# Another order for the first chunks of a fused sparse-attention and squared-ReLU MLP kernel

## The chip, the cores and the metric

The kernel runs on one core of a Trainium2 chip. The metric is the device time of one execution in microseconds. The kernel before took 374.07 us, the median of three runs (371.66 to 374.30).

## The reference

Attention with two sparsity patterns is followed by a two-layer MLP. Inputs and output are float32; the sizes are 8 batches, 8 heads, 576 positions, head dimension 64, and 512 to 2048 to 512 in the MLP.

```python
rel = pos[:, None] - pos[None, :]
mask_local   = (rel >= 0) & (rel < 32)                          # heads 0 to 3
mask_strided = (rel >= 0) & (pos[None, :] % 32 == pos[:, None] % 32)   # heads 4 to 7
scores = np.where(mask, (q @ k.T) / 8, -1e9)
attn = softmax(scores) @ v
x = attn.transpose(0, 2, 1, 3).reshape(4608, 512)   # tokens x model
h = np.maximum(x @ moe_w_in, 0.0)
out = (h * h) @ moe_w_out
```

## The kernel before, in words

**Attention.** Heads are taken in pairs, so a batch has four units: unit 4b and 4b+1 are local (pairs 0 and 1), unit 4b+2 and 4b+3 are strided. Each unit goes through steps, and each step is a function that issues instructions on several engines:

- `step_T` (line 175): TensorE (PE) transposes q or k in 6 or 8 pieces into a PSUM tile `pt`; ScalarE (ACT, L188) copies q out, VectorE (DVE, L190) copies k out.
- `step_S` (line 214): PE makes the scores in four `pt` banks. ACT takes the exponentials (L220) in four pieces, the first at once and the others one, two and three groups later; DVE multiplies with the mask (L226).
- `step_D` (line 251): PE multiplies the weights with v and a column of ones, in two parts (local) or three (strided). DVE takes the reciprocal (L262) and scales (L263).
- `step_E` (line 274): PE transposes the result, and ACT (units below 12) or DVE copies it into `xt`, the MLP's input (L280, L282).

**MLP.** Tokens are cut into nine chunks of 512. `mm1(c, ff)` (L294) is four matmuls of 128x512 into a tile `ph`; ACT takes the ReLU (L297) and DVE squares it into `g_sb` (L298). `mm2(c, i)` (L309) is four matmuls too, a quarter of the sum for one output block of 128 tokens; after the fourth quarter ACT copies the block to `y` (L313) and SyncE (SP) sends it out (L315). Both kinds are called groups here. There are 288, and g0, g1 and so on number them in program order. The pool `ps_h` holds two `ph` banks, `ps_y` one `py` bank, `ps_t` five `pt` banks.

**Order.** It is written out by hand. `first_steps` does the attention of batch 0, with 5 small matmuls of the identity (L326, `warm`) after each step from the first `step_D` on. Then the list `groups` runs: MM1 of chunk 0 (g0 to g15), MM1 of chunk 1 (g16 to g31), MM2 of chunk 0 (g32 to g47), and from g48 MM1 of chunk c in turn with MM2 of chunk c-1. The table `due` says how many attention steps stand ahead of each group: the steps of batch 1 lie between g9 and g16, those of batch 2 between g28 and g48, those of batch 3 between g48 and g80, and so on with 32 groups for each batch. A chunk may start when the batches it touches are done: chunk 1 needs batch 1, chunk 2 needs batches 1 and 2, chunk 3 needs batch 3.

**Loads.** `loads(b)` issues a batch's loads: float32 q, k and v on SP's queue, and q and k of the strided units on GpSimd's (POOL's) queue, which converts to bf16 on the way. POOL then casts the float32 tiles (L95, L123, L124, L139), one after the other in program order, and waits there for each load. `loads(1)` stands after the attention of batch 0, `loads(2)` at g8, `loads(3)` at g16, `loads(4)` at g48. In `loads(1)` POOL also issues the four quarters of `w_out` (L148); the four quarters of `w_in` are issued earlier (L144). The first load of batches 1 and 2 has a gate: POOL first copies one element of `w_in` (its third quarter) or `w_out` (its third quarter) into the tile (L86), so the load waits until that quarter has landed.

Of the kernel before, what the change touches and what calls it, by code (L numbers as in the profile page):

```python
# [8 lines left out]
FP32 = mybir.dt.float32  # L9
# [5 lines left out]
def kernel(  # L15
# [9 lines left out]
    nc = tc.nc  # L25
    B, H, S, D = q.shape
# [25 lines left out]
    ps_h = ctx.enter_context(tc.tile_pool(name="ps_h", bufs=2, space=PS))  # L52
    ps_y = ctx.enter_context(tc.tile_pool(name="ps_y", bufs=1, space=PS))
# [26 lines left out]
    def load_qk_local(u, eng, gate=None):  # L80
        b, p = units[u]
        s = st.setdefault(u, {})
        for name, src in (("q", q), ("k", k)):
            t = qk_st.tile([QL, 2, 6 * D], FP32, name=f"{name}_st")
            if gate is not None and name == "q":
                nc.gpsimd.tensor_copy(t[0:1, 0, 0:1], gate)  # L86
            eng.dma_start(out=t, in_=src[b, 2 * p:2 * p + 2]
                          .rearrange("h (p j) d -> p h (j d)", j=6))
            s[name + "f"] = t

    def cast_qk_local(u, copies):
        s = st[u]
        for name, copy in zip("qk", copies):
            t = qk_in.tile([QL, 6, 2, D], BF16, name=f"{name}_l")
            copy(t.rearrange("p j h d -> p h j d"),  # L95
                 s[name + "f"].rearrange("p h (j d) -> p h j d", j=6))
            s[name] = t

    def load_qk_str(u):
        b, p = units[u]  # L100
        s = st.setdefault(u, {})
        for name, src in (("q", q), ("k", k)):
            t = qk_in.tile([SP_, 2, NJ * D], BF16, name=f"{name}_s")
            nc.gpsimd.dma_start(out=t, in_=src[b, 2 * p:2 * p + 2]  # L104
                                .rearrange("h (p j) d -> p h (j d)", j=NJ))
            s[name] = t

    def v_slot(u):
        b, p = units[u]
        return (b * 2 + p % 2) % NV  # L110

    def load_v_local(u, eng):
        b, p = units[u]
        t = vl_sts[p]
        for hh in range(2):
            eng.dma_start(out=t[32:128, NL * hh:NL * (hh + 1), :],
                          in_=v[b, 2 * p + hh].rearrange("(t p) d -> p t d", p=QL))
        st.setdefault(u, {})["vf"] = t

    def cast_v_local(u):  # L120
        s = st[u]
        t = vls[v_slot(u)]
        nc.gpsimd.tensor_copy(t[:, :, :, 0:D].rearrange("p h t d -> p (h t) d"), s["vf"])  # L123
        nc.gpsimd.tensor_copy(  # L124
            t[0:32, :, 1:NL, 0:D],
            s["vf"][96:128].rearrange("p (h t) d -> p h t d", h=2)[:, :, 0:NL - 1, :])
        s["v"] = t

    def load_v_str(u, eng):
        b, p = units[u]  # L130
        t = v_st.tile([SP_, 2, NJ * D], FP32, name="v_st")
        eng.dma_start(out=t, in_=v[b, 2 * p:2 * p + 2]
                      .rearrange("h (p j) d -> p h (j d)", j=NJ))
        st.setdefault(u, {})["vf"] = t

    def cast_v_str(u, copy=None):
        s = st[u]
        t = vss[v_slot(u)]
        (copy or nc.gpsimd.tensor_copy)(t[:, :, 0:D], s["vf"].rearrange("p h (j d) -> p (h j) d", d=D))  # L139
        s["v"] = t  # L140
# [15 lines left out]
    def run_due(test):  # L156
        due = [x for x in pending if test(x)]
        for x in due:
            pending.remove(x)
        for x in sorted(due, key=lambda x: x[0]):  # L160
            x[2]()
# [138 lines left out]
    ys = {}  # L300

    def mm2(c, i, pool=None):
        j, part = divmod(i, 4)
        g = gs[c]
        if part == 0:
            ys[c] = (pool or ps_y).tile([128, 512], FP32, name="py" if pool is None else "ph")
        py = ys[c]
        for ff in range(4 * part, 4 * part + 4):
            nc.tensor.matmul(py, g[:, ff, 128 * j:128 * (j + 1)], w_out_b[:, ff, :],  # L309
                             start=(ff == 0), stop=(ff == 15))  # L310
        if part == 3:
            y = y_pool.tile([128, 512], FP32, name="y")
            nc.scalar.copy(y, py)  # L313
            r0 = 512 * c + 128 * j
            nc.sync.dma_start(out=out[r0:r0 + 128, :], in_=y)  # L315
# [12 lines left out]
    def first_steps():  # L328
        order = []
        for u in range(3):  # L330
            order += [T_(u, "q"), T_(u, "k"), S_(u)]
        order.append(lambda: cast_v_str(2, nc.scalar.copy))
        order += [T_(3, "q"), T_(3, "k"), S_(3)]
        order += [D_(0, 0), D_(0, 1), D_(1, 0), D_(1, 1), E_(0)]
        for u in (2, 3):
            order += [D_(u, 0), D_(u, 1), D_(u, 2), E_(u - 1)]
        order.append(E_(3))
        n = len(order)
        return [(fn, 0 if i < 12 else 5) for i, fn in enumerate(order)]

    def stream_steps(lo, hi, base):
        order = [T_(lo, "q"), T_(lo, "k"), T_(lo + 1, "q"), S_(lo), T_(lo + 1, "k")]
# [22 lines left out]
    def loads(b):  # L365
        u = 4 * b
        for i in range(2):
            load_qk_local(u + i, nc.sync, gate=gates.get(b) if i == 0 else None)
            load_v_local(u + i, nc.sync)
        load_v_str(u + 2, nc.sync)  # L370
        load_v_str(u + 3, nc.sync)
        w_out = load_w_out if b == 1 else (lambda i: None)
        load_qk_str(u + 2)
        cast_qk_local(u, pool2)
        cast_v_local(u)
        load_qk_str(u + 3)
        cast_qk_local(u + 1, pool2)
        w_out(0)
        cast_v_local(u + 1)
        w_out(1)  # L380
        cast_v_str(u + 2)
        w_out(2)
        cast_v_str(u + 3)
        w_out(3)

# [53 lines left out]
    NCH = T // 512  # L439
    steps, ends = stream_steps(4, 8, 0)  # L440
# [4 lines left out]
    starts = {}  # L445

    def add(c, kind, i, pool=None):
        if kind == 1:
            if i == 0:
                starts[c] = len(groups)  # L450
            groups.append(lambda: mm1(c, i))
        else:
            groups.append(lambda: mm2(c, i, pool))

    for c in range(2):
        for i in range(16):
            add(c, 1, i)
    for i in range(16):
        add(0, 2, i, ps_h)
    for c in range(2, NCH):  # L460
        for i in range(16):
            add(c, 1, i)
            add(c - 1, 2, i)
# [2 lines left out]

    due = [0] * (len(groups) + 1)
    done_prev, g_prev = 0, 0
    for b in range(1, B):
        g_end, s_end = starts[b], ends[4 * b + 3]  # L470
        g_prev += 9 if b == 1 else 12 if b == 2 else 0
        for g in range(g_prev, g_end + 1):
            due[g] = done_prev + (s_end - done_prev) * (g - g_prev) // (g_end - g_prev)
        done_prev, g_prev = s_end, g_end
    load_at = {max(8, starts[b - 2]): b for b in range(2, B)}
    done = 0
    for n, g in enumerate(groups):
        while done < due[n]:
# [38 lines left out]
```

## Time and profile before

| what | value |
|---|---|
| time, median of 3 runs | 374.07 us |
| time of the profiled execution | 371.82 us |
| its span, first to last instruction | 370.1 us |
| PE busy | 325.1 us, 88% of the span |
| DVE busy | 186.4 us, 50% |
| ACT busy | 177.8 us, 48% |
| POOL busy | 96.6 us, 26% |
| moved by DMA | 37.69 MB, mean 102 GB/s |

The span is cut into 40 slices of 9.25 us, with the busy tenths of each engine, the clock granted to PE and the DMA engines' share. Timeline rows give start and duration in microseconds, then engine, line, operation, tiles and count, and in brackets how long the engine was idle before and what released it. A window row gives the length, then for each engine busy time and count, then PE's granted clock, the DMA share and the rate in GB/s.

### The profile page before, as it was taken

To read this page: it belongs to the slowest core of one execution; us is meant where nothing else is said; L and a number is where in the kernel's file an instruction comes from. 1 tells how busy PE (TensorE), PEld (TensorE's weight loads), DVE (VectorE), ACT (ScalarE), POOL (GpSimd) and SP (SyncE) were. 2 spreads that over 40 slices of the span, in tenths; PEclk is the share of its full clock that TensorE was granted. 3 is DMA by queue.
4 is the path that set the end of the run, shared out by engine and by line. 5 is a ranking of instruction groups with operands and counts; after the bars stand their busy time and mean duration, and the time that the engine had idled before them with its cause. 6 is when DMAs were issued, how large, how long until landed. Compare 5 with 4: busy or idle time off the path is not lost.

```text
span 370.1 us, 6959 instructions
## 1 busy us (share of the span) xinstructions
PE 325.1 (88%) x2748; PEld 174.1 (47%) x2795; DVE 186.4 (50%) x446; ACT 177.8 (48%) x356; POOL 96.6 (26%) x126
## 2 busy tenths in 40 slices
PE   2589576489799989999999999989999999999995
PEld 1485343244455545454545555545445444444442
DVE  4465733645456576656666566656554622222200
ACT  3545533347454555555546555555554433443421
POOL 5354825900070570048007500820000000000000
PEclk9999955579899999999999999999999999999999
DMA  8999999930042970195219503910000011011021
GB/s 183 197 201 221 165 215 228 211 85 2 9 76 67 237 141 32 42 249 104 71 55 236 117 30 99 226 51 30 28 30 30 28 38 50 29 42 45 28 74 70
DMA packets 44193, 37.69 MB, mean 102 GB/s; under 512 B 22400, under 2 KB 37248, under 8 KB 44160
## 3 DMA queue, kind: packets, MB, share of 16 engines
q1 hardware_dynamic: 33280, 28.32, 30.4%
q0 software_dynamic: 10880, 8.92, 16.6%
q8 instruction: 22, 0.36, 0.4%
q14 instruction: 11, 0.09, 0.1%
HBM read 36.70 MB, written 9.44 MB: 125 GB/s over the span
## 4 chain that ended last, share of the span: by engine, by line
PE 73%; DVE 6%; DMA 4%; issue 3%; ACT 3%; POOL 3%; SPq 0%; POOLq 0%; ACTq 0%
PE ph L294 31%; PE py L309 25%; PE ph L309 7%; PE pt L251 3%; PE pt L214 3%; PE pt L175 3%; PE pt L274 2%; ACT r L297 2%; DMA w_out_b<-in_moe_w_out_dram 2%; DMA vl_st<-in_v_dram 2%; DVE g_sb L298 2%; DVE x_s L263 1%; DVE xt L282 1%; DVE kT L190 1%; POOL vs L139 1%
## 5 line engine op out<-in xcount | busy, mean ns | idle before, releaser
L294 PE MATMUL ph<-xt,w_in_b 128*128 128x512 bf16 x556 | 147.6, 390 | 2.7 <-DVE xt L282 1.0
L297 ACT ACTIVATE r<-ph 128x512 bf16<-128x512 f32 x144 | 86.0, 597 | 111.4 <-PE ph L294 108.9
L298 DVE TENSOR_TENSOR g_sb<-r 128x512 bf16<-128x512 bf16 x144 | 70.6, 492 | 127.8 <-ACT r L297 127.7
L309 PE MATMUL py<-w_out_b,g_sb 128*128 128x512 bf16 x427 | 111.5, 379 | 1.4 <-issue 0.5
L309 PEld LDWEIGHTS <-g_sb 128*128 128x128 bf16 x576 | 51.6, 98 | 55.0 <-issue 3.9
L294 PEld LDWEIGHTS <-w_in_b 128*128 128x128 bf16 x576 | 52.2, 100 | 52.5 <-issue 4.7
L220 ACT ACTIVATE e<-pt 72x288 bf16<-72x288 f32 (+1 forms) x128 | 48.6, 407 | 21.8 <-PE pt L214 21.5
L251 PEld LDWEIGHTS <-e 72*128 72x128 bf16 (+1 forms) x448 | 25.7, 104 | 22.6 <-DVE e L226 7.4
L95 POOL CAST q_l<-q_st 96x768 bf16<-96x768 f32 x14 | 11.7, 837 | 87.9 <-DMA q_st<-in_q_dram 85.6
L309 PE MATMUL ph<-w_out_b,g_sb 128*128 128x512 bf16 x122 | 30.8, 389 | 0.8 <-issue 0.5
L263 DVE TENSOR_TENSOR x_s<-pt,rinv 72x384 bf16<-72x384 f32 (+1 forms) x48 | 24.4, 509 | 1.7
L188 ACT COPY qT<-pt 128x576 bf16<-128x576 bf16 x32 | 20.3, 638 | 7.0 <-PE pt L175 6.0
L226 DVE TENSOR_TENSOR e<-e,mask_str 72x576 bf16<-72x576 bf16 x32 | 19.5, 610 | 7.3 <-ACT e L220 7.3
L313 ACT COPY y<-py 128x512 f32<-128x512 f32 x28 | 16.4, 586 | 10.3 <-PE py L309 9.5
L251 PE MATMUL pt<-vs,e 72*128 72x65 bf16 x256 | 16.2, 200 | 3.9 <-DVE e L226 3.9
L123 POOL CAST vl<-vl_st 128x768 bf16<-128x768 f32 x16 | 14.8, 927 | 18.2 <-DMA vl_st<-in_v_dram 14.6
L226 DVE TENSOR_TENSOR e<-e,mask_loc 128x576 bf16<-128x576 bf16 x32 | 15.4, 481 | 7.1 <-ACT e L220 7.0
L262 DVE RECIPROCAL rinv<-pt 96x6 f32<-96x6 f32 (+2 forms) x80 | 14.7, 183 | 8.4 <-PE pt L251 8.4
L214 PE MATMUL pt<-qT,kT 64*72 64x72 bf16 x256 | 8.6, 214 | 11.4 <-DVE kT L190 6.3
L104 POOL DMA_DIRECT2D q_s<-in_q_dram x16 | 11.3, 706 | 26.7 <-PE pt L175 25.1
L263 DVE TENSOR_TENSOR x_l<-pt,rinv 96x384 bf16<-96x384 f32 x32 | 17.7, 554 | 1.1
L139 POOL CAST vs<-v_st 72x1024 bf16<-72x1024 f32 x15 | 15.9, 1079 | 0.5
(54 smaller groups left out, 227.3 us busy)
## 6 DMA issues: line engine op xcount, KB each, us to landing
out_dram<-y SPq DMA_DIRECT2D x36, 256.0 KB
q_st<-in_q_dram SPq DMA_DIRECT2D x16, 288.0 KB
k_st<-in_k_dram SPq DMA_DIRECT2D x16, 288.0 KB
vl_st<-in_v_dram SPq DMA_DIRECT2D x32, 144.0 KB
v_st<-in_v_dram SPq DMA_DIRECT2D x16, 288.0 KB
q_s<-in_q_dram POOLq DMA_DIRECT2D x16, 144.0 KB, 6.1
k_s<-in_k_dram POOLq DMA_DIRECT2D x16, 144.0 KB, 6.5
w_in_b<-in_moe_w_in_dram POOLq DMA_DIRECT2D x4, 512.0 KB, 6.8
```

Source lines behind the costliest of these rows:

```text
L139: (copy or nc.gpsimd.tensor_copy)(t[:, :, 0:D], s["vf"].rearrange("p h (j d) -> p (h j) d", d=D))
L188: nc.scalar.copy(o, i)
L214: nc.tensor.matmul(banks[row][half][0:kn, w * i:w * (i + 1)], kT[rows, klo:klo + kn], qT[rows, w * t:w * (t + 1)], start=True, stop=True)
L220: nc.scalar.activation(e[0:kn, lo:lo + S // 2], banks[row][half][0:kn, 0:S // 2], AF.Exp, scale=scale)
L226: nc.vector.tensor_tensor(x, x, m.to_broadcast([kn, n, w]), op=ALU.mult)
L251: nc.tensor.matmul(po[:, n - n0, :], e[0:kn, pos(n):pos(n) + 128], rhs[0:kn, src(n), 0:D + 1], start=True, stop=True)
L263: nc.vector.tensor_tensor(x, po[0:w, 0:m, 0:D], rinv[0:w, 0:m].to_broadcast([w, m, D]), op=ALU.mult)
L294: nc.tensor.matmul(ph, w_in_b[:, kk, 128 * ff:128 * (ff + 1)], xt[kk][:, 512 * c:512 * (c + 1)], start=(kk == 0), stop=(kk == 3))
L297: nc.scalar.activation(r, ph, AF.Relu)
L298: later(1, lambda: nc.vector.tensor_tensor(g[:, ff, :], r, r, op=ALU.mult))
L309: nc.tensor.matmul(py, g[:, ff, 128 * j:128 * (j + 1)], w_out_b[:, ff, :], start=(ff == 0), stop=(ff == 15))
L313: nc.scalar.copy(y, py)
```

## The change

**Groups.** MM1 of chunk 0 is g0 to g15 as before, but MM2 of chunk 0 follows at once (g16 to g31), then MM1 of chunk 1 (g32 to g47), MM2 of chunk 1 (g48 to g63), MM1 of chunk 2 (g64 to g79), and from g80 the pairs as before. For the first three output blocks of chunk 0 the quarters are taken in turn, so three sums are open in PSUM at once, two in `ps_h` and one in `ps_y`; each quarter of `w_out` then serves three groups in a row.

**Attention.** The steps of batch 1 lie between g9 and g32, those of batch 2 between g32 and g56, those of batch 3 between g56 and g80. From g80 the table is the one before.

**Loads.** The quarters of `w_out` stand earlier on POOL's queue. `loads(3)` moves from g16 to g34, `loads(4)` from g48 to g58; later ones move by two groups.

**Batch 0.** ACT's cast of v of unit 2 moves behind all exponentials of unit 3. Of the 75 small matmuls 32 are left, 4 after each of the last eight steps.

```diff
-            ys[c] = (pool or ps_y).tile([128, 512], FP32, name="py" if pool is None else "ph")
-        py = ys[c]
+            ys[c, j] = (pool or ps_y).tile([128, 512], FP32, name="py" if pool is None else "ph")
+        py = ys[c, j]
...
-        order.append(lambda: cast_v_str(2, nc.scalar.copy))
         order += [T_(3, "q"), T_(3, "k"), S_(3)]
+        order.append(lambda: (run_due(lambda x: x[1] == 3), cast_v_str(2, nc.scalar.copy)))
...
-        return [(fn, 0 if i < 12 else 5) for i, fn in enumerate(order)]
+        return [(fn, 0 if i < n - 8 else 4) for i, fn in enumerate(order)]
...
         load_qk_str(u + 2)
+        w_out(0)
         cast_qk_local(u, pool2)
         cast_v_local(u)
         load_qk_str(u + 3)
+        w_out(1)
         cast_qk_local(u + 1, pool2)
-        w_out(0)
         cast_v_local(u + 1)
-        w_out(1)
+        w_out(2)
         cast_v_str(u + 2)
-        w_out(2)
         cast_v_str(u + 3)
         w_out(3)
...
-    for c in range(2):
+    def mm1_alone(c):
         for i in range(16):
             add(c, 1, i)
+
+    mm1_alone(0)
+    for part in range(4):
+        for j, pool in ((0, ps_h), (1, ps_h), (2, None)):
+            add(0, 2, 4 * j + part, pool)
+    for part in range(4):
+        add(0, 2, 12 + part, ps_h)
+    mm1_alone(1)
     for i in range(16):
-        add(0, 2, i, ps_h)
-    for c in range(2, NCH):
+        add(1, 2, i, ps_h)
+    mm1_alone(2)
+    for c in range(3, NCH):
...
+    ready = {1: 32, 2: 56}
+    load_at = {8: 2}
     for b in range(1, B):
-        g_end, s_end = starts[b], ends[4 * b + 3]
-        g_prev += 9 if b == 1 else 12 if b == 2 else 0
+        g_end, s_end = ready.get(b, starts[b]), ends[4 * b + 3]
+        if b == 1:
+            g_prev = 9
...
-    load_at = {max(8, starts[b - 2]): b for b in range(2, B)}
+        if b + 2 < B:
+            load_at[g_end + 2] = b + 2
```

DVE's order shows what stands between the attention steps of batch 1, since each `g_sb` row (L298) is one MM1 group and each `kTl` row (L190) belongs to a k transpose of a local unit. Before, from the tenth group of chunk 0:

```order
L298 TENSOR_TENSOR g_sb<-r 128x512 x10
L190 COPY kTl_110<-pt 128x576
L298 TENSOR_TENSOR g_sb<-r 128x512
L190 COPY kTl_111<-pt 128x576
L226 TENSOR_TENSOR e_112<-e_112,mask_loc 128x576 x2
L262 RECIPROCAL rinv<-pt 96x6
L263 TENSOR_TENSOR x_l<-pt,rinv 96x6x64
L298 TENSOR_TENSOR g_sb<-r 128x512
```

and now, the same place:

```order
L298 TENSOR_TENSOR g_sb<-r 128x512 x11
L190 COPY kTl_110<-pt 128x576
L298 TENSOR_TENSOR g_sb<-r 128x512 x3
L190 COPY kTl_111<-pt 128x576
L226 TENSOR_TENSOR e_112<-e_112,mask_loc 128x576
L298 TENSOR_TENSOR g_sb<-r 128x512 x2
L226 TENSOR_TENSOR e_112<-e_112,mask_loc 128x576
```

One group stood between the two k copies, now three do, and the last two squares of chunk 0 are done before the first `step_D` of batch 1; the rest of the batch stands among MM2 groups.

POOL's order in `loads(1)`, where L95 are the casts of local q and k, L123 and L124 of local v, L148 the quarters of `w_out`. Before:

```order
L104 DMA k_s<-in_k_dram 72x2x512
L95 CAST q_l<-q_st 96x2x6x64
L95 CAST k_l<-k_st 96x2x6x64
L123 CAST vl_101<-vl_st_107 128x12x64
L124 CAST vl_101<-vl_st_107 32x2x5x64
L104 DMA q_s<-in_q_dram 72x2x512
L104 DMA k_s<-in_k_dram 72x2x512
L95 CAST q_l<-q_st 96x2x6x64
L95 CAST k_l<-k_st 96x2x6x64
L148 DMA w_out_b<-in_moe_w_out_dram 128x4x512
```

and now:

```order
L104 DMA k_s<-in_k_dram 72x2x512
L148 DMA w_out_b<-in_moe_w_out_dram 128x4x512
L95 CAST q_l<-q_st 96x2x6x64
L95 CAST k_l<-k_st 96x2x6x64
L123 CAST vl_101<-vl_st_107 128x12x64
L124 CAST vl_101<-vl_st_107 32x2x5x64
L104 DMA q_s<-in_q_dram 72x2x512
L104 DMA k_s<-in_k_dram 72x2x512
L148 DMA w_out_b<-in_moe_w_out_dram 128x4x512
L95 CAST q_l<-q_st 96x2x6x64
L95 CAST k_l<-k_st 96x2x6x64
```

Two quarters of `w_out` now stand ahead of the casts of unit 5, the second pair of L95 rows, where before the first quarter stood behind them.

ACT's order at the end of batch 0's scores, where L220 are the exponentials of units 2 (`e_114`) and 3 (`e_115`), L188 the copy of q of unit 3, L139 the cast of v. Before:

```order
L139 CAST vs_103<-v_st 72x16x64
L220 ACTIVATE e_114<-pt 72x288
L188 COPY qT<-pt 128x576
L220 ACTIVATE e_114<-pt 72x288
L220 ACTIVATE e_115<-pt 72x288 x4
```

and now:

```order
L188 COPY qT<-pt 128x576
L220 ACTIVATE e_114<-pt 72x288 x2
L220 ACTIVATE e_115<-pt 72x288 x4
L139 CAST vs_103<-v_st 72x16x64
```

The cast, which stood ahead of the q copy and the exponentials, stands behind all of them.

## The prediction

> **What bounds the kernel now.** I read the page first: shares, then slices.
>
> ```profile
> PE 325.1 (88%) x2748; PEld 174.1 (47%) x2795; DVE 186.4 (50%) x446; ACT 177.8 (48%) x356; POOL 96.6 (26%) x126
> ...
> PE   2589576489799989999999999989999999999995
> ...
> PEclk9999955579899999999999999999999999999999
> DMA  8999999930042970195219503910000011011021
> ```
>
> PE is the bound from about slice 13 on, 9 tenths busy at the full granted clock. Before that it has holes (slices 5 to 8 and 10), and in slices 6 to 8 the granted clock is 5 tenths. The windows over those stretches say how bad each is.
>
> ```profile
> 29.84:38.30 8.46, 8.41 (x42) 3.83 (x41) 4.38 (x8) 5.83 (x10) 5.66 (x8) 1.00 1.11 218
> 38.30:48.00 9.70, 5.83 (x64) 3.10 (x64) 7.16 (x9) 4.07 (x10) 7.00 (x9) 0.85 1.14 169
> 48.00:76.40 28.40, 16.83 (x157) 10.33 (x159) 13.85 (x31) 9.56 (x21) 16.52 (x21) 0.50 1.15 217
> ...
> 89.00:119.25 30.25, 26.19 (x304) 15.28 (x309) 16.95 (x41) 15.80 (x37) 7.92 (x10) 0.94 0.23 47
> 119.25:154.50 35.25, 33.63 (x327) 18.01 (x328) 22.23 (x51) 19.50 (x41) 11.99 (x14) 1.00 0.53 115
> ```
>
> From 48.0 to 76.4 PE is busy 16.83 of 28.40 us, at clock 0.50: it waits between short dependent steps, and what it does takes double. The last row is the steady state: PE 33.63 of 35.25, with DVE at 63% and ACT at 55%. To price that I set the measured length against the full-rate work. A timeline gives the marks: g0, the first transpose of batch 1 (ten groups are done), g16, the first transpose of batch 2 (29 are done), g48 and g80.
>
> ```profile
> 29.84 8.80 PE L294 MATMUL ph<-xt,w_in_b 128*128 128x512 bf16 x39
> 38.47 0.42 PE L175 MATMUL pt<-ident,q_l 96*128 96x96 bf16 x6
> 38.73 0.42 PE L175 MATMUL pt<-ident,k_l 96*128 96x96 bf16 x6
> ...
> 42.21 0.43 PE L214 MATMUL pt<-qT,kTl 64*128 64x96 bf16 x12 [1.94 <-DVE kTl L190]
> ...
> 44.00 0.30 PE L214 MATMUL pt<-qT,kTl 64*128 64x96 bf16 x6 [1.00 <-DVE kTl L190]
> 44.80 0.67 PE L214 MATMUL pt<-qT,kTl 64*128 64x96 bf16 x6 [0.49 <-ACT e L220]
> ...
> 76.66 4.71 PE L294 MATMUL ph<-xt,w_in_b 128*128 128x512 bf16 x15 [0.22 <-issue]
> ...
> 88.98 0.42 PE L175 MATMUL pt<-ident,q_l 96*128 96x96 bf16 x6
> ...
> 119.84 1.27 PE L294 MATMUL ph<-xt,w_in_b 128*128 128x512 bf16 x4
> ...
> 155.58 0.81 PE L294 MATMUL ph<-xt,w_in_b 128*128 128x512 bf16 x3
> ```
>
> A group without attention is read from the tail of the chain that ended last, where ten groups follow one another:
>
> ```profile
> 298.52 0.86 PE ph L294 x4
> ...
> 307.15 0.86 PE ph L294 x4
> ```
>
> That is 8.63 / 10 = 0.863 us. From g48 to g80 pass 155.58 - 119.84 = 35.74 us; less 32 x 0.863 = 27.62 a whole batch of attention costs PE 8.1 us when it is spread over 32 groups. Now the ledger from g0 to g80, 125.74 us: work 80 x 0.863 + 3 x 8.1 = 93.3, lost 32.4. Of it 24.9 lie where batch 1 is squeezed (38.47 to 76.66 is 38.2 us for 6 groups and a batch, worth 13.3), 1.1 where chunk 1 begins at half clock (12.3 us for 13 groups, worth 11.2), and 6.4 in batch 2's stretch (30.9 us for 19 groups and a batch, worth 24.5). These 32.4 us are what the change can reach; what follows g80 has the same order before and after, so I carry it over unchanged.
>
> **The change part by part.** *Spreading batches 1 to 3.* Batch 1 gets 23 groups (g9 to g32) in place of 7, batch 2 gets 24 in place of 20, batch 3 gets 24 in place of 32. The order shows three groups between the two k copies where one stood, which covers the 1.94 and 1.00 us waits for `kTl`. All three batches together are worth the 32.4 us, less what new waits cost.
>
> *Where does chunk 0's MM1 start?* The rows of batch 0:
>
> ```profile
> 17.93 1.04 ACT L139 CAST vs<-v_st 72x1024 bf16<-72x1024 f32 x1 [2.67 <-DMA v_st<-in_v_dram]
> ...
> 18.86 0.71 POOL L124 CAST vl<-vl_st 32x640 bf16<-32x640 f32 x1
> ...
> 19.86 0.69 PE L214 MATMUL pt<-qT,kT 64*72 64x72 bf16 x16 [4.02 <-ACT qT L188]
> ```
>
> ```profile
> L263 DVE TENSOR_TENSOR x_s<-pt,rinv 72x384 bf16<-72x384 f32 (+1 forms) x48 | 24.4, 509 | 1.7
> L226 DVE TENSOR_TENSOR e<-e,mask_str 72x576 bf16<-72x576 bf16 x32 | 19.5, 610 | 7.3 <-ACT e L220 7.3
> L262 DVE RECIPROCAL rinv<-pt 96x6 f32<-96x6 f32 (+2 forms) x80 | 14.7, 183 | 8.4 <-PE pt L251 8.4
> ```
>
> The cast's 2.67 us wait and 1.04 us held PE 4.02 us at unit 3's scores. With the cast behind, the first `step_D` can start some 3 us sooner, and the next limit is the v cast of unit 1 on POOL, which ends at 18.86 + 0.71 = 19.57. From there DVE has eight scalings of 0.183 + 0.509 = 0.69 us and two masks of 0.61, 6.8 us, to 26.4. The small matmuls that go cost nothing on PE there, as DVE sets the pace; but fewer of them may warm the clock later, so I add 0.9: MM1 at 27.3, between 25.5 (some scalings already done) and 29.84 (no gain).
>
> *The wait that the change adds.* The DMA engines are busy 9 tenths until slice 8, so the first quarter of `w_out`, now ahead of batch 1's data, delays it. POOL's rows:
>
> ```profile
> 33.96 0.82 POOL L123 CAST vl<-vl_st 128x768 bf16<-128x768 f32 x1 [2.69 <-DMA vl_st<-in_v_dram]
> ...
> 37.00 0.82 POOL L95 CAST q_l<-q_st 96x768 bf16<-96x768 f32 x1
> 37.77 1.01 POOL L95 CAST k_l<-k_st 96x768 bf16<-96x768 f32 x1
> 38.73 0.77 POOL L148 DMA_DIRECT2D w_out_b<-in_moe_w_out_dram  x1
> ...
> 44.66 0.75 POOL L148 DMA_DIRECT2D w_out_b<-in_moe_w_out_dram  x1
> 50.93 0.18 POOL L86 CAST q_st<-w_out_b 1x1 f32<-1x1 bf16 x1 [5.52 <-DMA w_out_b<-in_moe_w_out_dram]
> ```
>
> ```profile
> 44.66 7.28 DMA w_out_b<-in_moe_w_out_dram
> ```
>
> Four quarters took from 38.73 to 44.66 + 7.28 = 51.94, 3.3 us each. The v cast at 33.96 already waits for its load, so it comes 0 to 3.3 us later; I take 2.6, near the upper end because the engines have no room. Behind it the issue of the second quarter adds 0.77, and the cast of q of unit 5 ends at 37.00 + 2.6 + 0.77 + 0.82 = 41.2. PE reaches that transpose after 12 groups and two transposes (0.26 each by the spacing of 38.47 and 38.73): 27.3 + 10.4 + 0.5 = 38.2. It waits 3.0 us, with chunk 0's last four MM1 groups queued behind it; bounds 0.4 and 5.0. An earlier start of MM1 only lengthens this wait.
>
> *Are the quarters in time?* The second is issued at about 40 and wanted at g19, near 50; the fourth at about 47 (some 2.3 us later than 44.66), lands by 54.5 with the 7.28 us of before, and is wanted at g25, near 59. I cost this at nothing. The cover is 4 us; if it is gone, PE waits up to 5 us. Batch 2's loads wait for the third quarter, which lands near 51 as before, and are wanted at g32, near 70. Batch 3's loads, now behind four output blocks on SP's queue, start near 69 and are wanted after g45, near 88.
>
> *The clock after the wait.* In the trace a similar stretch gave half clock: the idles of 1.94, 1.00 and 0.49 us above end in a six-matmul row of 0.67 us, against 0.43 for twelve before. The other such place shows the way back:
>
> ```profile
> 92.08 0.43 PE L214 MATMUL pt<-qT,kTl 64*128 64x96 bf16 x12 [0.44 <-DVE kTl L190]
> ...
> 95.30 0.34 PE L214 MATMUL pt<-qT,kTl 64*128 64x96 bf16 x7 [1.56 <-DVE kTl L190]
> 96.09 0.28 PE L214 MATMUL pt<-qT,kTl 64*128 64x96 bf16 x5 [0.46 <-ACT e L220]
> ...
> 98.80 1.51 PE L309 MATMUL ph<-w_out_b,g_sb 128*128 128x512 bf16 x4
> 100.14 0.34 PE L251 MATMUL pt<-vl,e 128*128 128x65 bf16 x6
> ```
>
> ```profile
> 95.20:99.90 4.70, 3.93 (x32) 2.16 (x34) 1.97 (x6) 2.29 (x7) 0.61 (x1) 0.64 0.00 0
> ```
>
> Four matmuls take 1.51 us at 98.80 (1.03 elsewhere), and six take 0.34 again at 100.14. So from 95.3 to 99.9, with PE busy 3.93 of 4.70 us, the clock is at half, then full: half of 4.6 is 2.3 us lost. I take 2.3 once; bounds 0 and twice that. The Trainium skill, "TensorE: Matmul & The Clock Gate", section "Part 1: The HAM clock gate", says that the clock falls to half after an idle window of about 3.4 us and comes back after about 3.4 us of sustained work. By that rule a 3.0 us wait would cost no clock, and the sum below would be 2.3 us less. The trace agrees with the way back but not with the fall: it came after idles none of which exceeded 1.94 us.
>
> *Density.* Batch 2's stretch lost 6.4 us at 19 groups a batch, and at 32 groups the loss is 0 by definition; in between, 23 to 24 groups give 4.2 a batch, 12.6 in all, as an upper bound. But the waits at 95 and the half clock behind them are 2.3 + 0.44 + 1.56 + 0.46 of the 6.4, and now a group lies there; some 1.4 us is left. I take 1.3 a batch, 4.0; lower bound 0. The shared `ph` banks (three sums open) and the extra `y` copies of ACT are inside this.
>
> *The sum.* 41.2 at the q transpose; 68 groups to g80, 58.7; attention left, 24.3 - 0.5 = 23.8; clock 2.3; density 4.0: g80 at 130.0 in place of 155.58. That is 25.6 us less. The profiled execution took 371.82, so 346.2; it stands 2.25 under the median of the three runs, of which I take half: **347.3 us**.
>
> **The rivals.** *Everything hidden.* The load is not delayed, the clock holds and no density loss: 347.3 - 2.6 - 2.3 - 4.0 = 338.4. For it speaks that ACT and DVE have a third of their time free in the steady state; against it the full DMA engines.
>
> *Waits in MM2 of chunk 0.* The quarters of `w_out` or the tighter chains stall PE once more: up to 5 us for the fourth quarter, or 8.6 more of density: 352 to 358. For it: the queues are full until slice 8. Against it: every quarter has some microseconds of cover.
>
> *The clock stays at half (the other side).* If the gaps between groups keep PE at 0.50 from the q transpose on, each group costs 0.863 more. Over batches 1 and 2 (g12 to g55, 44 groups) that is 38.0 us in place of the 2.3: 383. It ends slower than before from 34 such groups on. For it: from 48.0 to 76.4 the clock never came back at 59% busy. Against it: at 95 to 100 it came back at 84% busy, and the new order has a group of 0.863 us between any two steps.
>
> *The change does not do what it says.* If MM2 of chunk 0 could not fill the gaps of batch 1, because its weights all land only at the end of the queue, PE would stand from the end of MM1 near 46 to 54.5, 8.5 us, rewarm once more, 2.3, and find batch 1 clumped behind it, 4.2 of density: 15 us more, 362. Against it: the first quarter is issued near 28, before most of batch 1's data.
>
> **How the numbers follow.** The forecast 0.67; everything hidden 0.12; waits in MM2 0.13; the change not doing what it says 0.02; half clock 0.06, of which 0.02 for a half clock that ends after about 30 groups and so comes out level, 0.04 for one that lasts through both batches. The likeliest case alone spans 343 to 352. The range takes in most of the hidden and the waiting case, to the bounds of the unknown costs: 339 to 358; it leaves out the half clock, the 362 and the outermost part of the hidden case. About 1% is what a measurement of this kernel can tell from no change, so faster means under 370.3. Faster: 0.67 + 0.12 + 0.13 + 0.02 = 0.94; within 1%: 0.02; slower: 0.04.
>
> **What would show it.** The granted clock at 1.0 in nearly all slices after the fourth; one stretch of a few microseconds near 38 to 46 with PE idle behind the q cast on POOL; the DVE wait for `kTl` gone from PE's list; g80 (MM1 of chunk 3) near 130; the tail from there 214 to 215 us long as before; batch 0 ending some 2.5 us sooner. I am wrong in kind if the half clock lasts over 10 us, or if PE waits for `w_out` by name; wrong in size if the density loss is 0 or over 8.

## The result and the profile after

The changed kernel took 353.56 us, the median of four (349.53 to 355.01), beside 372.92 us for the kernel before on the same chip: a ratio of 0.945, with a 95% interval of 0.937 to 0.953. Executions more than 1.5% above the fastest of their kernel are left out of the ratios here, so a ratio can differ a little from that of the medians. The forecast was 347.3 with a range of 339 to 358. The profiled execution is the fastest of them: 349.53 us, with a span of 347.8 us.

The page of the changed kernel, shares and slices:

```profile
PE 315.1 (91%) x2752; PEld 166.6 (48%) x2752; DVE 183.5 (53%) x446; ACT 177.3 (51%) x356; POOL 97.6 (28%) x126
...
PE   2679769878899999999999999999999999999995
...
PEclk9999999999999999999999999999999999999999
DMA  7999999896209991330494039300000000100021
```

The three slices at half clock are gone. The holes of PE that are left are shallow: 6 to 9 tenths in slices 5 to 11, where before there were 4 to 9. The windows are cut where a batch's stretch of groups ends: g32, g48, g56 and g80 begin at the right edges. The first number is the length, then come busy time and count of PE, PE's weight loads, DVE, ACT and POOL, the granted clock, the DMA share and GB/s.

```profile
41.07:68.60 27.53, 23.88 (x263) 12.94 (x260) 15.97 (x35) 13.73 (x30) 16.63 (x22) 1.00 1.07 205
68.60:93.75 25.15, 20.33 (x233) 11.28 (x233) 15.60 (x35) 17.81 (x38) 13.98 (x17) 1.00 0.70 141
93.75:104.35 10.60, 9.82 (x116) 5.55 (x113) 6.88 (x18) 4.83 (x12) 0.00 (x0) 1.00 0.07 26
104.35:133.69 29.34, 27.80 (x299) 15.11 (x295) 20.59 (x51) 18.60 (x41) 16.09 (x18) 1.00 0.96 210
```

In the first row, batch 1 with 20 groups beside it, PE is busy 23.88 of 27.53 us at full clock. The squeezed stretch of the kernel before had 16.83 of 28.40 at clock 0.50. The second row is the new weak place: MM1 of chunk 1 beside the first two thirds of batch 2, with PE idle for 4.8 of 25.15 us. From the timeline of PE, the marks and the longest waits:

```profile
27.61 8.86 PE L294 MATMUL ph<-xt,w_in_b 128*128 128x512 bf16 x40
...
40.80 0.43 PE L175 MATMUL pt<-ident,q_l 96*128 96x96 bf16 x6 [2.08 <-POOL q_l L95]
...
42.03 0.43 PE L214 MATMUL pt<-qT,kTl 64*128 64x96 bf16 x12
...
45.86 0.43 PE L214 MATMUL pt<-qT,kTl 64*128 64x96 bf16 x12 [1.31 <-DVE kTl L190]
...
48.78 0.20 PE L251 MATMUL pt<-vl,e 128*128 128x65 bf16 x1 [1.36 <-DVE e L226]
...
76.38 0.43 PE L214 MATMUL pt<-qT,kTl 64*128 64x96 bf16 x12 [1.05 <-DVE kTl L190]
...
133.69 0.81 PE L294 MATMUL ph<-xt,w_in_b 128*128 128x512 bf16 x3
```

MM1 starts at 27.61, the q transpose of unit 5 runs at 40.80 after a wait of 2.08 us, and twelve matmuls take 0.43 us again at 42.03, so the clock held here. g80 stands at 133.69 in place of 155.58, 21.9 us sooner, and the tail is 347.8 - 133.69 = 214.1 us. All that PE waited for between 27.6 and 133.7 us, with the sum, the times and the longest:

```profile
PE pt L214 <- DVE kTl L190: 3.8, 5, 1.3
PE pt L251 <- DVE e L226: 3.3, 3, 1.5
PE pt L214 <- DVE kT L190: 2.7, 4, 1.4
PE pt L175 <- POOL q_l L95: 2.1, 1, 2.1
PE pt L274 <- DVE x_s L263: 0.9, 2, 0.5
```

No row names `w_out`. Four of the five name DVE, which is busy only some 6 tenths there. DVE's own timeline shows why it is late (the bracket is DVE's idle time before the row):

```profile
74.87 0.78 DVE L298 TENSOR_TENSOR g_sb<-r 128x512 bf16<-128x512 bf16 x1 [1.57 <-ACT r L297]
75.57 0.75 DVE L190 COPY kTl<-pt 128x576 bf16<-128x576 bf16 x1
```

L298 is the square of the MM1 group that PE has just done, L190 the k copy that PE waits for at 76.38. In DVE's order the square stands first, so DVE idles 1.57 us for ACT's ReLU of that group, squares it, and only then copies k, at 75.57. The copy's own input was ready before that: PE's transpose of k ran at 74.04 and took 0.42 us.

### The profile page after: what moved, and what is told of

Read it like the earlier page. It is cut to its first block, busy times and chain, and to the rows that moved or that the text cites. A ratio compares the mean times of both kernels' runs of the same rounds, so it can differ in the third digit from the quotient of the medians.

```text
span 347.8 us, 6912 instructions
## 1 busy us (share of the span) xinstructions
PE 315.1 (91%) x2752; PEld 166.6 (48%) x2752; DVE 183.5 (53%) x446; ACT 177.3 (51%) x356; POOL 97.6 (28%) x126
## 4 chain that ended last, share of the span: by engine, by line
PE 70%; DVE 12%; ACT 6%; DMA 6%; issue 2%; SPq 1%; POOL 1%; ACTq 0%; POOLq 0%
PE ph L294 27%; PE py L309 23%; PE ph L309 8%; DVE g_sb L298 4%; DMA vl_st<-in_v_dram 3%; PE pt L214 3%; ACT r L297 3%; PE pt L251 3%; PE pt L175 3%; DMA k_st<-in_k_dram 2%; PE pt L274 2%; DVE e L226 2%; DVE kTl L190 1%; DVE xt L282 1%; DVE x_s L263 1%
## 5 line engine op out<-in xcount | busy, mean ns | idle before, releaser
L298 DVE TENSOR_TENSOR g_sb<-r 128x512 bf16<-128x512 bf16 x144 | 69.8, 486 | 113.3 <-ACT r L297 113.2
L309 PE MATMUL py<-w_out_b,g_sb 128*128 128x512 bf16 x400 | 102.8, 379 | 0.0
L294 PEld LDWEIGHTS <-w_in_b 128*128 128x128 bf16 x576 | 50.1, 98 | 46.9 <-issue 0.2
L220 ACT ACTIVATE e<-pt 72x288 bf16<-72x288 f32 (+1 forms) x128 | 48.8, 407 | 16.9 <-PE pt L214 16.6
L309 PE MATMUL ph<-w_out_b,g_sb 128*128 128x512 bf16 x176 | 42.8, 379 | 0.0
L95 POOL CAST q_l<-q_st 96x768 bf16<-96x768 f32 x14 | 11.9, 849 | 72.4 <-DMA q_st<-in_q_dram 68.8
L188 ACT COPY qT<-pt 128x576 bf16<-128x576 bf16 x32 | 20.4, 638 | 9.1 <-PE pt L175 8.1
L123 POOL CAST vl<-vl_st 128x768 bf16<-128x768 f32 x16 | 14.7, 922 | 21.0 <-DMA vl_st<-in_v_dram 21.0
L226 DVE TENSOR_TENSOR e<-e,mask_str 72x576 bf16<-72x576 bf16 x32 | 17.8, 558 | 3.8 <-ACT e L220 3.7
L313 ACT COPY y<-py 128x512 f32<-128x512 f32 x25 | 14.7, 586 | 8.8 <-PE py L309 8.8
L313 ACT COPY y<-ph 128x512 f32<-128x512 f32 x11 | 6.4, 586 | 20.9 <-PE ph L309 18.6
L139 POOL CAST vs<-v_st 72x1024 bf16<-72x1024 f32 x15 | 16.9, 1152 | 0.4
L251 PE MATMUL pt<-vl,e 128*128 128x65 bf16 x192 | 11.8, 199 | 3.8 <-DVE e L226 2.8
```

The source lines that it names most:

```text
L188: nc.scalar.copy(o, i)
L220: nc.scalar.activation(e[0:kn, lo:lo + S // 2], banks[row][half][0:kn, 0:S // 2], AF.Exp, scale=scale)
L226: nc.vector.tensor_tensor(x, x, m.to_broadcast([kn, n, w]), op=ALU.mult)
L251: nc.tensor.matmul(po[:, n - n0, :], e[0:kn, pos(n):pos(n) + 128], rhs[0:kn, src(n), 0:D + 1], start=True, stop=True)
L294: nc.tensor.matmul(ph, w_in_b[:, kk, 128 * ff:128 * (ff + 1)], xt[kk][:, 512 * c:512 * (c + 1)], start=(kk == 0), stop=(kk == 3))
L298: later(1, lambda: nc.vector.tensor_tensor(g[:, ff, :], r, r, op=ALU.mult))
```

## The experiments

Two questions were open. **Where did the 19 us come from:** from batch 1's wider stretch (my account), from the earlier start of MM1, or from the chunks' order? **Where did the missing 6 us go:** to the clock after the q wait, or to DVE's order? In the expectations theory A is the account held when the run was made, and the others are its rivals. The kernel before had medians of 372.49 us (first four runs), 371.95 (next four), 372.15 (three more) and 372.61 (the last) beside them.

### The changed kernel once more

No edit: it asks whether the executions of one kernel differ by the clock.

> The changed kernel once more, as the measure for the others and for a second trace. In its first trace the clock was full throughout and the time 349.5 us; other executions took 353 to 355 us at a mean clock of 0.98 to 0.99. Theory A (a short spell at half clock, started by the wait for the cast of q of unit 5, comes and goes between executions): where the mean clock of the trace is under 1, the half clock begins within some microseconds behind the wait at 38 to 41 us, lasts some 5 us, and the time is 353 us. Rival B (the later executions lose time in many small waits): clock at 1 in all stretches and the longer time spread over g80 and after.

Measured: 354.02 us (348.38 to 355.36, n = 4), ratio 0.943 (0.933 to 0.953). The profiled execution took 353.57 with a mean granted clock of 0.985. Its PE timeline and windows:

```profile
41.17 0.43 PE L175 MATMUL pt<-ident,q_l 96*128 96x96 bf16 x6 [3.81 <-POOL q_l L95]
...
43.16 1.89 PE L294 MATMUL ph<-xt,w_in_b 128*128 128x512 bf16 x4
...
80.45 0.23 PE L251 MATMUL pt<-vl,e 128*128 128x65 bf16 x1 [1.89 <-DVE e L226]
...
80.97 1.90 PE L294 MATMUL ph<-xt,w_in_b 128*128 128x512 bf16 x4
```

```profile
41.00:47.00 6.00, 5.31 (x36) 2.43 (x36) 1.71 (x3) 2.92 (x6) 5.81 (x8) 0.72 1.14 171
80.00:85.00 5.00, 4.55 (x28) 2.34 (x29) 2.59 (x7) 1.60 (x4) 0.77 (x2) 0.50 0.72 145
```

Four matmuls take 1.89 us in place of 1.03 at two places of this execution: behind the q wait, as forecast, and behind the `e` wait at 80, which I had not priced. A mean clock of 0.985 over 351.8 us is, if all the shortfall is half clock, 2 x 0.015 x 351.8 = 10.6 us at half rate and 5.3 us of delay, an estimate. The two executions of the changed kernel at clock 1.00 took 348.38 and 349.53, those at 0.982 to 0.993 took 352.74 to 355.36. So the clock term is real, it is paid in most executions and not in all, and the trace with which the last section was read is one that did not pay it. The longer q wait here is no later cast but an earlier start: MM1 begins at 26.28 in this trace, and the q transpose runs at 41.17, nearly where it ran before (40.80).

### Batch 1 squeezed again

```diff
-    ready = {1: 32, 2: 56}
+    ready = {1: 16, 2: 56}
```

> Batch 1's attention back between g9 and g16, all else as in the changed kernel (MM2 of chunk 0 still behind MM1 of chunk 0). Theory A (the loss was the squeezed attention, with its waits and the half clock): PE stands and falls to half clock from about 42 to 75 us again, and most of the gain goes: 366 to 374 us. Rival B (the order of the chunks and the earlier weights made the gain, the spreading little): 350 to 357 us.

Measured: 369.45 us (366.52 to 371.77, n = 10), ratio 0.991 (0.988 to 0.995). Its stretch of batch 1:

```profile
50.00:76.50 26.50, 15.46 (x150) 9.30 (x150) 12.56 (x28) 9.57 (x21) 16.85 (x21) 0.56 1.12 212
```

The order of the chunks, the places of `w_out` and batch 0 are those of the change, and 15.4 us of its 18.5 us are gone (369.45 against 354.02 and 372.49 in the same session). The window reads as it did before the change: PE busy 15.46 of 26.50 at clock 0.56. The line also does two other things: batch 2's steps now lie between g16 and g56, 40 groups in place of 24, and `loads(3)` moves from g34 to g18. The trace says where the time goes all the same: from the first transpose of batch 1 at 37.96 to g16 at 77.83 pass 39.9 us, worth 13.3 by the prediction's prices, so 26.6 are lost there, 24.9 before the change. From g16 to g64 (133.07) only 3.0 are lost: 55.2 us for 48 groups, batch 2 and a third of batch 3, worth 52.2. Theory A stands: the gain is batch 1's groups.

### The earlier start alone

```diff
-        order.append(lambda: cast_v_str(2, nc.scalar.copy))
         order += [T_(3, "q"), T_(3, "k"), S_(3)]
+        order.append(lambda: (run_due(lambda x: x[1] == 3), cast_v_str(2, nc.scalar.copy)))
...
-        return [(fn, 0 if i < 12 else 5) for i, fn in enumerate(order)]
+        return [(fn, 0 if i < n - 8 else 4) for i, fn in enumerate(order)]
```

These lines were put into the kernel before.

> The kernel before with the change in batch 0 alone (the cast behind the exponentials, 32 small matmuls in place of 75). Theory A (MM1 of chunk 0 starts 2.2 us sooner, but the next things wanted, the casts of batch 1 on POOL, come at a time set by the loads): MM1 at 27.6, then most of it is given back, 0 to 1 us faster than before. Rival B (all that follows moves with it): 2.2 us faster. Rival C (fewer small matmuls leave the clock at half when MM1 starts): no change or 1 us slower.

Measured: 371.95 us (369.21 to 374.31, n = 10), ratio 0.999 (0.996 to 1.002): nothing.

```profile
27.26 8.87 PE L294 MATMUL ph<-xt,w_in_b 128*128 128x512 bf16 x39
...
38.66 0.43 PE L175 MATMUL pt<-ident,q_l 96*128 96x96 bf16 x6 [2.02 <-POOL q_l L95]
```

MM1 starts 2.6 us sooner than 29.84, and the q transpose of unit 5 runs at 38.66. In the kernel before the same transpose is the third of batch 1's:

```profile
38.99 0.42 PE L175 MATMUL pt<-ident,q_l 96*128 96x96 bf16 x6
```

So 0.3 us are left of the 2.6. POOL's cast of that q, which follows the loads, sets the point, and the gain turns into a wait of 2.02 us. Theory A again; not rival C, since MM1's first 39 matmuls take 8.87 us here and 8.80 before, both at the full clock.

### The quarters of w_out at their old places

```diff
-        w_out(0)
         cast_qk_local(u, pool2)
         cast_v_local(u)
         load_qk_str(u + 3)
-        w_out(1)
         cast_qk_local(u + 1, pool2)
+        w_out(0)
         cast_v_local(u + 1)
-        w_out(2)
+        w_out(1)
         cast_v_str(u + 2)
+        w_out(2)
```

> The quarters of w_out back to their places behind the casts of unit 5, all else as in the changed kernel. Theory A (the first quarters delay unit 5's q by about 2 us, and the quarters have some microseconds of cover): the wait for that cast shrinks from 2.1 us to under 0.5, MM2 of chunk 0 waits for no quarter or under 1 us, 1 to 3 us faster than the changed kernel. Rival B (the quarters are wanted at once): MM2 waits at g16 to g25 for weights by name, 2 to 6 us slower.

Measured: 353.76 us (353.29 to 354.24, n = 4), ratio 0.950 (0.946 to 0.955): no change in time. But the trace is not the same:

```profile
38.41 0.42 PE L175 MATMUL pt<-ident,q_l 96*128 96x96 bf16 x6
...
45.44 0.43 PE L214 MATMUL pt<-qT,kTl 64*128 64x96 bf16 x12 [1.89 <-DVE kTl L190]
...
48.40 1.90 PE L309 MATMUL ph<-w_out_b,g_sb 128*128 128x512 bf16 x4
```

The q wait is gone, 2.4 us are won there, and then `kTl` is late by 1.33 (at 41.03) and 1.89 us, `e` by 1.36, and the clock falls at 48.4. Neither theory as stated: the wait that was removed was real, and waits for DVE took its place. PE waits for no quarter of `w_out` here either, so their earlier places bought nothing. That pointed to DVE's order.

### The square one group later

```diff
-        later(1, lambda: nc.vector.tensor_tensor(g[:, ff, :], r, r, op=ALU.mult))
+        later(2, lambda: nc.vector.tensor_tensor(g[:, ff, :], r, r, op=ALU.mult))
```

The square of a group is now put on DVE one group later, when ACT's ReLU is long done, so nothing that DVE does next stands behind a wait for ACT.

> The changed kernel with the squares of MM1 given to DVE two groups after their ReLU in place of one, so that a k copy no longer stands behind a square that waits for the ReLU of the group just before. Theory A (the loss beyond the forecast is the chain k transpose, square, k copy, scores): PE's waits for kTl and kT between 27 and 135 us fall from 6.5 us (3.8 and 2.7) to under 3, 2 to 4 us faster than the changed kernel. Rival B (the squares are in place in time and DVE itself is slow there, its copies and squares lengthened while POOL casts): waits and time as before, within 1 us.

Measured: 344.23 us (341.99 to 347.32, n = 6), ratio 0.925 (0.920 to 0.929), which is 9.3 us below the changed kernel by the medians and some 7 by the ratios; the intervals don't meet. Between the profiled executions, at clock 0.999 and 1.00, it is 6.4 us; the median holds more, as three of these six executions kept the clock at 0.999, and of the changed kernel's nine two. It is more than theory A gave it. DVE's timeline at the same k copy as in the section above:

```profile
73.34 0.43 DVE L298 TENSOR_TENSOR g_sb<-r 128x512 bf16<-128x512 bf16 x1 [0.40 <-ACT r L297]
74.56 0.76 DVE L190 COPY kTl<-pt 128x576 bf16<-128x576 bf16 x1 [0.79 <-PE pt L175]
```

The copy is now released by its own input, PE's transpose, after 0.79 us of idle. Over the whole span DVE's idle time ahead of squares, waiting for ACT (us and times), was in the changed kernel, and is here:

```profile
  ACT r L297: 113.2, 119
```

```profile
  ACT r L297: 74.9, 68
```

What PE waits for in the first 130 us:

```profile
PE pt L251 <- DVE e L226: 2.7, 2, 1.3
PE pt L175 <- POOL q_l L95: 2.6, 1, 2.6
PE pt L214 <- ACT e L220: 1.3, 2, 0.7
PE ph L294 <- ACT xt L282: 0.8, 1, 0.8
...
PE pt L214 <- DVE kTl L190: 0.4, 1, 0.4
```

`kTl` has fallen from 3.8 to 0.4 us (and `kT` from 2.7 to 0.5). g80 comes at 130.35, 3.3 us sooner, and the tail is 211.05 us, 3.1 us shorter than in the changed kernel: the squares were in the way in the steady part too, which I had carried over as untouched. The same line put into three other kernels (below) was worth 6.9, 5.9 and 9.1 us by the medians, 5 to 9 by the ratios.

### The mask and the exponentials at once, alone and with the late square

```diff
         expo(0, 0)
+        if 4 <= u < 16:
+            expo(0, 1)
+            masks(0)
+            later(1, lambda: (expo(1, 0), expo(1, 1), masks(1)), u)
+            return
         later(1, lambda: expo(0, 1), u)
```

This asks whether the wait for `e`, 3.3 us, is a price of its own.

> The changed kernel with the exponentials and masks of units 4 to 15 issued sooner: two pieces and the first mask at once, the rest one group later, in place of one, two, three and four groups later. Theory A (with 23 groups a batch the delayed mask is wanted before its turn): PE's wait for the mask (e, 3.3 us) goes, 1.5 to 3.5 us faster. Rival B (ACT then takes the ReLUs later, and the groups wait for their banks): the wait moves to PE's ph matmuls, no change or slower.

> The two edits together, late squares and early exponentials. Theory A (two separate waits): the gains add, 4 to 7 us faster than the changed kernel, 346 to 349 us, and the half clock is seen less. Rival B (one chain, the freed time is taken by the next wait): no more than the better of the two.

Measured: alone 352.38 us (350.07 to 353.38, n = 6), ratio 0.947 (0.942 to 0.951), no difference from the changed kernel that its spread lets one tell; with the late square 345.50 (344.08 to 349.02, n = 6), ratio 0.930 (0.925 to 0.935), no better than the late square alone. With the edit alone:

```profile
47.00 0.43 PE L214 MATMUL pt<-qT,kTl 64*128 64x96 bf16 x12 [2.53 <-DVE kTl L190]
```

```profile
44.62 0.48 DVE L226 TENSOR_TENSOR e<-e,mask_loc 128x576 bf16<-128x576 bf16 x1 [0.87 <-ACT e L220]
```

The wait for `e` has left PE's list, and those for `kTl` and `kT` have grown from 3.8 and 2.7 to 5.1 and 4.7 us: the mask that now runs sooner stands ahead of the k copy, waits there for ACT, and the copy runs at 46.20 in place of 45.06. The wait moved, and the edit doesn't pay, neither alone nor with the late square.

### The quarters of the sums not in turn

```diff
-    for part in range(4):
-        for j, pool in ((0, ps_h), (1, ps_h), (2, None)):
-            add(0, 2, 4 * j + part, pool)
-    for part in range(4):
-        add(0, 2, 12 + part, ps_h)
+    for i in range(16):
+        add(0, 2, i, ps_h)
```

> The changed kernel with the output blocks of chunk 0 one after the other, one sum open at a time, so that the fourth quarter of w_out is wanted at g19 in place of g25. Theory A (the fourth quarter lands near 53 us): PE waits for w_out by name at g18 or g19, near 52 us, for 0 to 3 us, and the time is 0 to 3 us longer. Rival B (the open sums hold banks that MM1 and the y copies want): 1 to 3 us faster.

Measured: 353.09 us (352.20 to 354.66, n = 6), ratio 0.950 (0.946 to 0.953).

```profile
55.13 1.02 PE L309 MATMUL ph<-w_out_b,g_sb 128*128 128x512 bf16 x4 [1.07 <-DMA w_out_b<-in_moe_w_out_dram]
```

Without the three open sums PE does wait for a quarter of `w_out` by name, for 1.07 us, as theory A had it; in the time it can't be told from the changed kernel.

### One stream of attention steps, alone and with the late square

In the changed kernel batch 1's steps are one list and those of batches 2 to 7 another, so unit 8 starts only when unit 7 has ended. Here they are one list, and the units overlap there as elsewhere.

```diff
-    steps, ends = stream_steps(4, 8, 0)
-    more, more_ends = stream_steps(8, 4 * B, len(steps))
-    steps = steps + more
-    ends.update(more_ends)
+    steps, ends = stream_steps(4, 4 * B, 0)
```

> The changed kernel with the attention of batches 1 to 7 in one list of steps, so that the first transposes and scores of batch 2 stand among batch 1's last steps in place of a new start at g32. Theory A (of the 10.1 us beyond the full-rate work between the q transpose of unit 5 and g80, 6.9 lie in batch 2, 68.6 to 104.35 us, because its first steps stand alone and wait for each other): that stretch becomes 3 to 5 us shorter, the time 3 to 5 us less than the changed kernel. Rival B (it is batch 2's place among MM1 groups, whose squares and ReLUs hold its copies up): the waits for kT and kTl only move, within 1.5 us. Rival C (batch 2's data come too late for the earlier steps): PE waits for q_l or k_l of units 8 and 9 by name near 60 to 68 us.

> One list of steps and late squares together. Theory A (two causes, a restart at batch 2 and the squares ahead of the copies everywhere): 340 to 342 us, 2 to 4 us under late squares alone. Rival B (late squares have already taken away what the restart costs): 343 to 345 us, as late squares alone.

Measured: alone 348.70 us (344.99 to 351.21, n = 6), ratio 0.934 (0.928 to 0.939), 4.9 us under the changed kernel by the medians, though the intervals of the ratios touch. With the late square 342.81 (339.08 to 343.72, n = 6), ratio 0.919 (0.914 to 0.924), 1.4 us under the late square alone, with overlapping intervals. In the first the waits at 72.81, 76.38 and 79.40, where batch 2 starts, are gone, while that for `kT` has grown from 2.7 to 3.9 us; part of them is what the late square removes too, so the two edits don't add up. The 342.81 lies between what theory A and rival B gave, and settles neither. The second shows the clock's caprice:

```profile
40.42 0.43 PE L175 MATMUL pt<-ident,q_l 96*128 96x96 bf16 x6 [2.52 <-POOL q_l L95]
...
42.51 1.91 PE L294 MATMUL ph<-xt,w_in_b 128*128 128x512 bf16 x4
```

After a wait of 2.52 us the clock fell here, and after one of 2.65 us at the same place it held with the late square alone. With the start alone it fell behind the wait of 2.02 us, and in the changed kernel it held behind one of 2.08.

### The old places of w_out with the late square

The edits of the fourth and fifth runs together.

> Late squares with the quarters of w_out back behind the casts of unit 5. Theory A (with w_out late the wait for the cast had gone, but its place was taken by the waits for kTl behind squares and by the half clock that they started; without them the removal pays): 341 to 343 us and the clock full from 40 to 55 us. Rival B (the earlier w_out costs nothing anyway, some other wait ends last there): 343 to 346 us.

Measured: 344.67 us (344.18 to 345.81, n = 6), ratio 0.927 (0.923 to 0.932): no better than the late square alone. PE's and ACT's timelines at g32:

```profile
69.08 0.59 PE L294 MATMUL ph<-xt,w_in_b 128*128 128x512 bf16 x1 [3.95 <-ACT xt L282]
...
69.94 1.91 PE L294 MATMUL ph<-xt,w_in_b 128*128 128x512 bf16 x4
```

```profile
67.90 0.59 ACT L313 COPY y<-ph 128x512 f32<-128x512 f32 x1 [6.80 <-DMA out_dram<-y]
68.38 0.64 ACT L282 COPY xt<-pt 128x576 bf16<-128x576 bf16 x1
```

The rival: the q wait of 2.6 us is nearly gone (0.32), PE reaches g32 four microseconds sooner, and waits there 3.95 us for an `xt` copy that stands on ACT behind the copy of an output block. That copy finds no free `y` buffer (there are three) for 6.80 us: chunk 0's first block, copied by 57.7, is issued on SP only at 60.41, behind batch 2's loads, and its buffer is free at 67.8. Then the clock falls.

### The four together

One stream, late square, old places of `w_out`, and two more `y` buffers:

```diff
-    y_pool = ctx.enter_context(tc.tile_pool(name="y_pool", bufs=3))
+    y_pool = ctx.enter_context(tc.tile_pool(name="y_pool", bufs=5))
```

> Late squares, one list of steps, w_out behind the casts of unit 5, and five y buffers in place of three. With late squares and late w_out, ACT's copy of chunk 0's last output block waited 6.8 us for a y buffer whose out transfer was queued behind batch 2's loads, the copy to xt behind it kept PE waiting 4.0 us at g32, and the clock fell to half. Theory A (each of these waits had only passed its place on to the next, and with the last of them gone the removal of the cast's wait pays): PE waits neither for q of unit 5 nor for xt at g32, the clock stays full from 37 to 75 us in most executions, 335 to 340 us. Rival B (batch 2's casts come at a time set by the loads, and the earlier steps now wait for them): PE waits for q_l or k_l of units 8 or 9 by name between 55 and 68 us, 340 to 344 us.

Measured: 340.66 us (339.66 to 343.04, n = 6), ratio 0.915 (0.911 to 0.919): the lowest median of all, 12.9 us under the changed kernel and 32 under the kernel before. Its interval overlaps that of one stream with the late square (0.914 to 0.924), so what the last two edits add is not shown. PE's waits from 27 to 133 us and g80:

```profile
PE pt L214 <- DVE kT L190: 2.5, 4, 0.8
PE pt L175 <- POOL q_l L95: 1.3, 1, 1.3
PE pt L251 <- DVE e L226: 1.3, 1, 1.3
PE pt L214 <- ACT e L220: 0.7, 1, 0.7
```

```profile
127.97 0.81 PE L294 MATMUL ph<-xt,w_in_b 128*128 128x512 bf16 x3
```

The waits that theory A meant to remove are gone, that for `xt` behind ACT's `y` copy among them. But the time lies just above theory A's range and inside the rival's, the clock is full in the profiled execution alone (0.985 to 0.995 in the other five), and the wait that the rival named is there: at 65.98 the q transpose of unit 9, which the one stream has moved forward, waits 1.33 us for POOL's cast. Both theories are right in part.

## Why the prediction was right, and where its steps were wrong

- **The kind.** Batch 1's squeeze was 24.9 of the 32.4 us lost before, and most of them can be won by giving it 23 groups. Shown: put back, the squeeze takes back 15.4 of 18.5 us, with 26.6 lost in batch 1's stretch. By the same ledger the changed kernel loses 12.8 us from g0 to g80, where 32.4 were lost before. (The holes that the prediction reads in slices 5 to 8 and 10 of the page before lie in 5 to 9 and 11; nothing in the sum rests on this.)
- **The start and the load.** MM1 at 27.3: 27.61. The v cast of unit 4 delayed by 2.6: it ran at 36.12 in place of 33.96, 2.2. The transpose at 41.2 after a wait of 3.0: 40.80 and 2.08 in the profiled execution, 41.17 and 3.81 in the other. That MM1 started so near the forecast is partly luck: with the same batch 0 it started between 26.17 (old places of `w_out` with the late square) and 29.31 (batch 1 squeezed) in the other traces. It matters little, for an earlier start only lengthens this wait, which the start alone shows (ratio 0.999).
- **The quarters.** In time, at no cost: no wait for them by name. Shown from the other side by the sums not in turn, with 1.07 us.
- **The clock, 2.3.** Zero in the profiled execution; in the other one the fall behind the q wait that I had forecast, and a second behind `e` at 80. In the sum for one execution the term was too large, in the sum for the median too small by a spell. The Trainium skill's rule ("TensorE: Matmul & The Clock Gate", "Part 1: The HAM clock gate") of an idle window of about 3.4 us again fails: the clock fell after idles none of which exceeded 1.89 us, with the old places of `w_out`; of the waits shown, only the 3.81 us of the second trace and the 3.95 at g32 are as long as the rule asks. The same section of the Trainium skill says that the window runs freely, and that the instant of the way up depends on where in it the first matmul lands. If the way down depends on the place too, which no run here tests, the 2.52 us that lost the clock and the 2.65 us that kept it would agree.
- **Density, 4.0: the step that failed.** From 41.07 to 133.69 the loss is 10.4 us by the prediction's own prices: 3.0 in batch 1's stretch (27.53 us, worth 24.6), 6.9 in batch 2's (35.75, worth 28.8), 0.5 in batch 3's (29.34, worth 28.8). By the prediction's own test, over 8, it was wrong in size. I had taken batch 1's 1.94 and 1.00 us waits for `kTl` as covered because three groups now stand between the k copies, and batch 2's waits near 95 with their half clock because a group now lies there, and so cut batch 2's old loss of 6.4 to 1.3 (6.4 less these waits is 1.6, not the 1.4 of the text). But each of these groups also puts a square on DVE, ahead of the copy, that waits for ACT: the groups that were to hide the wait make part of it. The sign that I had named, the wait for `kTl` gone from PE's list, did not come: 5.2 us from g0 to g80 before, 3.8 now. Putting the square one group later, an edit that changes nothing else, took that wait to 0.4. From the q transpose at 41.73 to g80 at 130.35 the density loss is then 6.1 by the same prices, so the squares are 4.3 of the 6.4 us that the term lacked. The other 2.1 stay open; what PE still waits for there is above all `e` (2.7 us for DVE's mask, 1.3 for ACT's exponentials).
- **The tail, 214 to 215.** 214.1, as it was. That it can't be reached was true of this change only; the late square cut it to 211.05.

Together: 346.2 for the profiled execution became 349.53, by -0.4 (load), -2.3 (clock), +6.4 (density) and -0.4 (tail). The median, 353.56, lies another 4.0 higher, which is what the executions with a lower clock show. It lies in the range, but above the 343 to 352 of the likeliest case and in that of the rival with tighter chains, which had the right size and half the right cause: the chains were tighter, but no quarter of `w_out` was late, and of PE's waits 4.8 us lie beside MM1 of chunk 1 and only 1.0 beside MM2 of chunk 0. That the profiled execution came within 3.3 us of its 346.2 is in part luck: the density term was short by 6.4, and the 2.3 of the clock were not paid there.

Open is which instant decides whether the clock falls: no run here set the length of a wait and its place apart.

## What to carry to other kernels

Work put between two dependent steps covers a wait only if it adds nothing ahead of the second step on the engine that the wait is for: read that engine's order, not only PE's. On an engine that works in order, an instruction that waits for another engine's fresh result belongs behind those whose inputs are ready; recording the square one group later was worth 5 to 9 us in four kernels, where moving the quarters of `w_out` back was worth nothing. And removing one wait early in a chain (the q cast) showed nothing in the time while others stood behind it (the k copy, the `y` buffer); with these removed as well the median fell from 342.81 to 340.66, which suggests that it then pays, but does not show it.

## What the runs showed of the hardware

The granted clock fell to half behind waits of 1.4 to 4 us, and not in each execution of the same program, so a single profile can miss a term that the median holds. In the second trace of the changed kernel it was at half for 3.4 us behind the q wait (0.72 over 6.00 us) and for at least 5 us behind the `e` wait.

DVE's square of 128x512 has a median of 0.43 us, but beside POOL's casts it can take more. In the changed kernel's trace 106 squares ran beside no cast, and none took over 0.43 us; the other 38 had a median of 0.58, and one took 1.36. The rows show one of 1.04. This was seen in the trace, not tried by itself, and what it costs PE is open.

```profile
44.09 1.04 DVE L298 TENSOR_TENSOR g_sb<-r 128x512 bf16<-128x512 bf16 x1 [0.75 <-ACT r L297]
```

```profile
43.82 2.21 POOL L139 CAST vs<-v_st 72x1024 bf16<-72x1024 f32 x2
```
